# A two-layer MLP with squared ReLU: the first loads and transposes in another order

## The chip, the core and the metric

The kernel runs on one core of a Trainium2 chip. The metric is the device time of one execution in microseconds (us); the figure for a kernel is the median of several runs. The core has five engines that run their own instruction streams side by side: TensorE (PE, matrix products; its weight loads are listed as PEld), VectorE (DVE), ScalarE (ACT), GpSimd (POOL) and SyncE (SP). DMA transfers are issued from the queues of SP, ACT and POOL and are carried by 16 DMA engines. SBUF is the memory on the chip with 128 partitions, PSUM the accumulator memory that PE writes, here eight banks of 512 fp32 columns.

## The reference

```python
B, S, D, F = 1, 2048, 576, 4608      # all inputs bf16
h = jnp.einsum("bsd,df->bsf", x, w1) + b1
r = jnp.where(h > zero, h, zero)
h = r * r
out = jnp.einsum("bsf,fd->bsd", h, w2) + b2
```

x is (1, 2048, 576), w1 is (576, 4608), w2 is (4608, 576).

## The kernel before

**Tiling.** The 2048 rows of x are taken in four blocks of 512 (SB). The hidden dimension F has 36 tiles of 128 (NFT). D = 576 is four full contraction tiles of 128 (NK) and a rest of 64. For the first layer the kernel needs x transposed, so that D lies on the partitions; this is the tile xTw of a block, with nine windows of 64 rows that are held twice, once on each half of the partitions (dup_windows, L117-120, two DVE copies).

**The two ways of the first layer.** Of the 36 hidden tiles, 4 (G) are "full" tiles: a_full computes them with 128-row contractions (w1n, the first 512 columns of w1 in four k tiles of 128 rows) and one step for the last 64 rows of w1 (w1n8), in pairs: the first of a pair on the lower 64 rows of the array, the second on the upper (L202-206). The other 32 are done by a_rows (L179-193) as 16 pairs of 64-row contractions, nine for each, on both halves of the array at once; their weights are w1_h, named w_h in the profile. evac_h (L174-177) finishes a hidden tile: ACT adds b1 and applies ReLU, DVE squares. b1 as a column, b1T, comes from one PE transpose of b1_rows (make_b1T, L164-167).

**The second layer.** phase_t computes the last 128 output columns transposed and turns them by a DMA transpose; phase_b computes the other 448 columns for each 128 rows, adds b2 and stores.

**Order of the work (L309-329).** Block 0: a_full with the order "k_outer", then a_rows. Block 1: a_rows, a_full. Then the second layer of both; then the same for blocks 2 and 3. `keep` holds every instruction to the order of the program on its engine; the order around the start is written out by hand, and each engine takes its instructions strictly in that order.

**The start.** PE runs seven warm-up matmuls on constants (L61-63). Block 0 of x is loaded as four row tiles of 128 x 576 (x_sb, load_x L71-72) and transposed by PE (x_transpose, L145-149), five transposes for each row tile: four of 128 columns, and one of the last 128 columns (E3). PSUM banks hold two halves of 256 rows; x_copies (L151-159) moves them to SBUF on DVE and ACT in turn. SP loads x 0, w1n 0, w1n 1, x 3, w1n 2, w1n 3, then w_h in pieces for the two halves of the partitions (L294-303), with the two w1n8 loads (L77-79) behind the first two pieces. ACT loads x 1 and x 2. POOL makes the identity matrix, zeroes b1_rows and loads b1 and a column of b2 (L94-102).

In a_full's "k_outer" branch (L220-250) matmuls on the halves (`part(h, k)`, L227, four matmuls of 256 columns for the four full tiles) stand between the transposes:

```python
for j in range(2):
    for k in range(NK):
        x_transpose(j, k)
...
x_copies(0)
part(0, 0)
for k in range(NK + 1):
    x_transpose(2, k)
part(0, 1)
part(0, 2)
for k in range(NK + 1):
    x_transpose(3, k)
x_copies(1)
dup_windows(0)
part(0, 3)
part(1, 0)
make_b1T()
```

Then come part(1, 1) to part(1, 3), the two row pairs (L203, L205), and a_rows with L188 and L190.

Of the kernel before, what the change touches and what calls it, by code (L numbers as in the profile page):

```python
# [11 lines left out]
BF16 = mybir.dt.bfloat16  # L12
FP32 = mybir.dt.float32
# [4 lines left out]
def kernel(  # L18
# [9 lines left out]
    nc = tc.nc  # L28
    keep = tc.keep_in_program_order
    P = 128  # L30
    H = 64
    x2 = x.flatten_outer_dims()
    out2 = out.flatten_outer_dims()
    S, D = x2.shape
    F = w1.shape[1]
    NFT = F // P
    NC = D // H
    NK = NC // 2
    G = 4
    GW = G * P  # L40
# [4 lines left out]
    RT = SB // P  # L45
    DT = P
    DM = D - DT

    const = ctx.enter_context(tc.tile_pool(name="const", bufs=1))
    wpool = ctx.enter_context(tc.tile_pool(name="wpool", bufs=1))  # L50
# [5 lines left out]
    ps_h = ctx.enter_context(tc.tile_pool(name="ps_h", bufs=4, space=PSUM))  # L56
    ps_o = ctx.enter_context(tc.tile_pool(name="ps_o", bufs=4, space=PSUM))

    wps = ps_o.tile([P, 512], FP32, name="wps", tag="po")
    ones = nc.const_aps.tensor(1.0, [P, 512], BF16)  # L60
    WARM = [512] * 6 + [128]  # L61
    for i, n in enumerate(WARM):
        keep(nc.tensor.matmul(wps[:, 0:n], lhsT=ones[:, 0:P], rhs=ones[:, 0:n], start=True, stop=True))  # L63

    xs = const.tile([P, RT, D], BF16, name="x_sb")
    w1n = wpool.tile([P, NK, GW], BF16, name="w1n")
    w1n8 = wpool.tile([P, G // 2, P], BF16, name="w1n8")
    w1_h = wpool.tile([P, NC, FH], BF16, name="w1_h")
    w1_v = w1.rearrange("(c p) f -> p c f", p=H)

    def load_x(eng, rt):  # L71
        keep(eng.dma_start(out=xs[:, rt, :], in_=x2[rt * P:(rt + 1) * P, :]))  # L72

    def load_w1n(eng, k):
        keep(eng.dma_start(out=w1n[:, k, :], in_=w1[k * P:(k + 1) * P, 0:GW]))  # L75

    def load_w1n8(eng, h):  # L77
        src = w1[NK * P:D, 0:GW].rearrange("p (i h f) -> p i h f", h=2, f=P)
        keep(eng.dma_start(out=w1n8[h * H:(h + 1) * H, :, :], in_=src[:, :, h, :]))

    def load_w1(eng, h, j0, j1):
        keep(eng.dma_start(out=w1_h[h * H:(h + 1) * H, :, j0 * P:j1 * P],
                      in_=w1_v[:, :, GW + h * FH + j0 * P:GW + h * FH + j1 * P]))

    load_x(nc.sync, 0)
    load_x(nc.scalar, 1)
    load_w1n(nc.sync, 0)
    load_x(nc.scalar, 2)
    load_w1n(nc.sync, 1)
    load_x(nc.sync, 3)  # L90
    for k in range(2, NK):
        load_w1n(nc.sync, k)

    ident = const.tile([P, P], BF16, name="ident")  # L94
    make_identity(nc, ident[:])
    b1_rows = const.tile([P, P], BF16, name="b1_rows")
    nc.gpsimd.memset(b1_rows[:], 0.0)
    nc.gpsimd.dma_start(out=b1_rows[0:NFT, :], in_=b1.rearrange("(ft p) -> ft p", p=P))
    b2_col = const.tile([P, 1], BF16, name="b2_col")
    nc.gpsimd.dma_start(out=b2_col[:], in_=b2[DM:D].rearrange("(d o) -> d o", o=1))  # L100
    b2T = const.tile([P, 1], FP32, name="b2T")
    nc.gpsimd.tensor_copy(out=b2T[:], in_=b2_col[:])
    warm = const.tile([P, 1], FP32, name="warm")
    keep(nc.scalar.activation(out=warm[:], in_=nc.const_aps.tensor(0.0, [P, 1], FP32), func=ACT.Relu))

    E3, O, SPC, E = 0, 1, 5, 6
    LO_W = [O, O + 1, O + 2, O + 3, E, E + 1, E + 2, E3, SPC]
# [20 lines left out]

    w2_sb = wpool.tile([P, NFT, D], BF16, name="w2_sb")
    w2_view = w2.rearrange("(ft p) d -> p ft d", p=P)  # L130
    W2CH = 9

    def load_w2(c):
        keep(nc.sync.dma_start(out=w2_sb[:, c * W2CH:(c + 1) * W2CH, :], in_=w2_view[:, c * W2CH:(c + 1) * W2CH, :]))
# [3 lines left out]
    alloc_xT(0)  # L138
    xT0 = xT_blk[0]
    HS = SB // 2  # L140
    tb_po = [ps_o.tile([P, 2, HS], BF16, name="tb", tag="po") for _ in range(2)]
    tb_ph = [ps_h.tile([P, 2, HS], BF16, name="tb", tag="ph") for _ in range(4)]
    half_banks = [tb_ph, None]

    def x_transpose(j, k):  # L145
        h, q = divmod(j, 2)
        qc = slice(q * P, (q + 1) * P)
        bank, slot, c0 = (half_banks[h][k], 0, k * P) if k < NK else (half_banks[h][2], 1, D - P)
        keep(nc.tensor.transpose(bank[:, slot, qc], xs[:, j, c0:c0 + P], ident[:]))  # L149

    def x_copies(h):  # L151
        hc = slice(h * HS, (h + 1) * HS)
        for k in range(NK):
            src = half_banks[h][k][:, 0, :]
            if k % 2 == 0:
                keep(nc.vector.tensor_copy(out=xT0[:, O + k, hc], in_=src))  # L156
            else:
                keep(nc.scalar.copy(out=xT0[:, O + k, hc], in_=src))  # L158
        keep(nc.vector.tensor_copy(out=xT0[:, E3, hc], in_=half_banks[h][2][:, 1, :]))


    b1T = const.tile([P, NFT], FP32, name="b1T")

    def make_b1T():  # L164
        b1T_ps = ps_o.tile([P, P], BF16, name="b1T_ps", tag="po")
        keep(nc.tensor.transpose(b1T_ps[:], b1_rows[:], ident[:]))  # L166
        keep(nc.vector.tensor_copy(out=b1T[:], in_=b1T_ps[:, 0:NFT]))

# [26 lines left out]
    def a_full(sb, order):  # L195
        xT = xT_blk[sb]
        banks = []
        for g in range(G):
            pool, tag = (ps_o, "po") if g < 2 else (ps_h, "ph")
            banks.append(pool.tile([P, SB], FP32, name="pn", tag=tag))  # L200

        def pair(i, start, stop):  # L202
            keep(nc.tensor.matmul(banks[2 * i][:], lhsT=w1n8[0:H, i, :], rhs=xT[0:H, SPC, :],  # L203
                             start=start, stop=stop, skip_group_check=order == "k_outer"))
            keep(nc.tensor.matmul(banks[2 * i + 1][:], lhsT=w1n8[H:P, i, :], rhs=xT[H:P, E3, :],  # L205
                             start=start, stop=stop, skip_group_check=order == "k_outer"))

        def full(g, k, start, stop):
            keep(nc.tensor.matmul(banks[g][:], lhsT=w1n[:, k, g * P:(g + 1) * P], rhs=xT[:, O + k, :],  # L209
                             start=start, stop=stop))  # L210

        if order == "rows_first":
            for i in (1, 0):
                pair(i, True, False)
            for g in (2, 3, 0, 1):
                for k in range(NK):
                    full(g, k, False, k == NK - 1)
                evac_h(sb, banks[g], g)
        else:
            if order == "k_outer":  # L220
                tb_new = [ps_h.tile([P, 2, HS], BF16, name="tb", tag="ph") for _ in range(2)]
                half_banks[1] = tb_new + tb_po

                def part(h, k):
                    hc = slice(h * HS, (h + 1) * HS)
                    for g in range(G):
                        keep(nc.tensor.matmul(banks[g][:, hc], lhsT=w1n[:, k, g * P:(g + 1) * P],  # L227
                                              rhs=xT[:, O + k, hc], start=(h == 0 and k == 0), stop=False,
                                              skip_group_check=True))

                for j in range(2):
                    for k in range(NK):
                        x_transpose(j, k)
                for j in range(2):
                    x_transpose(j, NK)
                x_copies(0)
                part(0, 0)
                for k in range(NK + 1):
                    x_transpose(2, k)
                part(0, 1)  # L240
                part(0, 2)
                for k in range(NK + 1):
                    x_transpose(3, k)
                x_copies(1)
                dup_windows(0)
                part(0, 3)
                part(1, 0)
                make_b1T()
                for k in range(1, NK):
                    part(1, k)  # L250
            else:
                for g in (2, 3, 0, 1):
                    for k in range(NK):
                        full(g, k, k == 0, False)
            for i in (1, 0):
                pair(i, False, True)
                evac_h(sb, banks[2 * i], 2 * i)
                evac_h(sb, banks[2 * i + 1], 2 * i + 1)
# [35 lines left out]
    for (j0, j1) in [(0, 1), (1, 2), (2, 4), (4, 6), (6, 8), (8, 10), (10, 12)]:  # L294
        load_w1(nc.sync, 0, j0, j1)
        load_w1(nc.sync, 1, j0, j1)
        if j0 == 0:
            load_w1n8(nc.sync, 0)
            load_w1n8(nc.sync, 1)
    load_xT(1)  # L300
    for (j0, j1) in [(12, 14), (14, 16)]:
        load_w1(nc.sync, 0, j0, j1)
        load_w1(nc.sync, 1, j0, j1)
    keep(nc.sync.dma_start(out=b2_bc[:], in_=b2.partition_broadcast(P)))
    for c in (0, 2, 1, 3):
        load_w2(c)
    load_xT(2)

    alloc_hT(0)  # L309
    a_full(0, "k_outer")  # L310
    a_rows(0, 12, 1)
    alloc_hT(1)
# [47 lines left out]
```

## Time and profile before

| | |
|---|---|
| median of 8 runs | 290.93 us (290.62 to 291.45) |
| the profiled execution | 290.9 us, its span 289.1 us |
| PE busy | 285.3 us, 99% of the span |
| DVE, ACT, POOL busy | 78.5, 96.6, 2.2 us |
| first transposes of x (L149) start | 3.73 us |
| first matmul of a_rows (L188) starts | 9.82 us |
| read from HBM, written | 11.36 MB, 2.36 MB |

The landings of the first loads, each from the trace (issue start, us to landing):

| load | queue | issued | to landing |
|---|---|---|---|
| x 0, x 1 | SP, ACT | 0.73, 0.73 | 2.9, 2.8 |
| w1n 0, x 2 | SP, ACT | 1.20, 1.2 | 3.2, 3.0 |
| w1n 1 | SP | 1.69 | 3.9 |
| x 3 | SP | 2.16 | 3.7 |
| w1n 2, w1n 3 | SP | 2.65, 3.12 | 3.6, 3.7 |
| first two w_h pieces | SP | 3.60, 4.3 | 3.5, 3.5 |
| two w1n8 loads | SP | 5.04, 5.7 | 3.0, 2.5 |

How to read the lines: times are microseconds from the start of the span. A line of the timeline gives start, length, engine, line of the kernel, operation, output<-input by the program's names, shape and count. The chain of waits follows the execution back from its last instruction, at each step to what released it; "issue" in it is time in which an engine waited for nothing that the profile shows, and SPq is SP's issuing of a DMA.

### The profile page before, as it was taken

Reading aid. Unit: us, or ns where it says so; the run is one execution under the profiler, and the core shown is the slowest. Engines: PE = TensorE matmul, PEld = TensorE weight load, DVE = VectorE, ACT = ScalarE, POOL = GpSimd, SP = SyncE. Lnnn points to the kernel's source line nnn. Section 1 sums busy time; section 2 is a strip of 40 time slices with the busy share of each in tenths; the row PEclk is TensorE's granted clock in tenths of the full one; section 3 lists DMA queues with packets and bytes.
Section 4 is the critical chain, followed back from the end, with each engine's and each line's share of the span. In section 5 each row is a group of like instructions: output and inputs, shape, how many; then the busy total and the mean of one; then the engine's idle time right before and its main releaser. Section 6 shows DMA issues by size and latency. Waiting matters only on the chain.

```text
span 289.1 us, 4698 instructions
## 1 busy us (share of the span) xinstructions
PE 285.3 (99%) x2032; PEld 139.0 (48%) x2032; DVE 78.5 (27%) x176; ACT 96.6 (33%) x154; POOL 2.2 (1%) x10
## 2 busy tenths in 40 slices
PE   8999999999999999999999999999999999999996
PEld 4544444444444555555544444444444455555555
DVE  1644554444500200000025444444440001100001
ACT  3666666666500000000027666666670000000000
POOL 3000000000000000000000000000000000000000
PEclk9999999999999999999999999999999999999999
DMA  7999999300001100000000000000000110000000
GB/s 198 222 250 195 328 387 207 68 0 2 0 18 30 42 16 18 16 16 18 16 16 2 1 2 0 2 0 2 0 2 0 36 39 16 16 16 20 32 16 18
DMA packets 31605, 16.52 MB, mean 57 GB/s; under 512 B 15700, under 2 KB 31584, under 8 KB 31584
## 3 DMA queue, kind: packets, MB, share of 16 engines
q1 hardware_dynamic: 31232, 15.91, 21.7%
q10 hardware_dynamic: 288, 0.30, 0.4%
q8 instruction: 16, 0.26, 0.4%
q14 instruction: 5, 0.04, 0.0%
q0 software_dynamic: 64, 0.01, 0.0%
HBM read 11.36 MB, written 2.36 MB: 47 GB/s over the span
## 4 chain that ended last, share of the span: by engine, by line
PE 97%; DMA 1%; SPq 1%; issue 0%; DVE 0%
PE ph L188 42%; PE po L289 38%; PE pt L270 11%; PE pn L209 4%; DMA w1n<-in_w_dram 1%; PE pn L227 1%; PE ph L190 1%; PE pn L203 1%; SPq L75 0%; SPq L72 0%; DVE o_sb L291 0%; PE tb L149 0%; PE b1T_ps L166 0%; PE pn L205 0%
## 5 line engine op out<-in xcount | busy, mean ns | idle before, releaser
L188 PE MATMUL ph<-xTw,w_h 64*128 64x512 bf16 x576 | 124.6, 376 | 0.0
L190 PE MATMUL ph<-xTw,w_h 64*128 64x512 bf16 x576 | 124.6, 376 | 0.0
L289 PE MATMUL po<-w_sb,hT 128*128 128x448 bf16 (+2 forms) x612 | 109.4, 341 | 0.0
L176 ACT ACTIVATE r<-ph,b1T 128x512 bf16<-128x512 f32 x128 | 81.0, 684 | 41.7 <-PE ph L190 41.7
L188 PEld LDWEIGHTS <-w_h 64*128 64x128 bf16 x576 | 54.1, 94 | 68.3
L289 PEld LDWEIGHTS <-hT 128*128 128x128 bf16 x612 | 58.5, 98 | 51.0
L177 DVE TENSOR_TENSOR hT<-r 128x512 bf16<-128x512 bf16 x144 | 61.2, 425 | 75.9 <-ACT r L176 75.3
L190 PEld LDWEIGHTS <-w_h 64*128 64x128 bf16 x576 | 54.1, 94 | 0.0
L291 DVE TENSOR_TENSOR o_sb<-po,b_bc 128x448 bf16<-128x448 f32 (+2 forms) x17 | 10.2, 597 | 125.8 <-PE po L289 125.8
L270 PE MATMUL pt<-hT,w_sb 128*128 128x512 bf16 x144 | 31.4, 379 | 0.0
L176 ACT ACTIVATE r<-pn,b1T 128x512 bf16<-128x512 f32 x16 | 10.3, 687 | 61.0 <-PE pn L205 59.6
L270 PEld LDWEIGHTS <-w_sb 128*128 128x128 bf16 x144 | 14.1, 98 | 17.0
L273 ACT ACTIVATE oT<-pt,b2T 128x512 bf16<-128x512 f32 x4 | 2.7, 687 | 28.3 <-PE pt L270 28.3
L209 PE MATMUL pn<-xTw,w1n 128*128 128x512 bf16 x48 | 10.9, 379 | 0.0
L209 PEld LDWEIGHTS <-w1n 128*128 128x128 bf16 x48 | 4.5, 98 | 6.0 <-issue 0.8
L227 PE MATMUL pn<-xTw,w1n 128*128 128x256 bf16 x32 | 4.2, 273 | 0.2
L63 PE MATMUL wps<-const-bfloat16-1.0 128*128 128x512 bf16 (+1 forms) x7 | 2.8, 581 | 0.8 <-PEq L344 0.8
L227 PEld LDWEIGHTS <-w1n 128*128 128x128 bf16 x32 | 2.9, 98 | 1.0 <-DMA w1n<-in_w_dram 0.4
L119 DVE COPY xTw<-xTw 64x2048 bf16<-64x2048 bf16 x4 | 2.8, 690 | 0.2
L156 DVE COPY xTw<-tb 128x256 bf16<-128x256 bf16 x4 | 1.1, 292 | 6.3 <-PE tb L149 6.3
L120 DVE COPY xTw<-xTw 64x2048 bf16<-64x2048 bf16 x4 | 2.8, 688 | 0.1
L158 ACT COPY xTw<-tb 128x256 bf16<-128x256 bf16 x4 | 1.3, 375 | 3.3 <-PE tb L149 3.3
(23 smaller groups left out, 15.2 us busy)
## 6 DMA issues: line engine op xcount, KB each, us to landing
w_sb<-in_w_dram SPq DMA_DIRECT2D x4, 1296.0 KB, 12.0
w_h<-in_w_dram SPq DMA_DIRECT2D x14, 288.0 KB, 6.2
out_dram<-o_sb SPq DMA_DIRECT2D x15, 112.0 KB, 1.7
w_h<-in_w_dram SPq DMA_DIRECT2D x4, 144.0 KB, 3.5
w1n<-in_w_dram SPq DMA_DIRECT2D x4, 128.0 KB, 3.6
out_dram<-ot SPq DMA_DIRECT2D x4, 128.0 KB, 2.0
x_sb<-in_x_dram ACTq DMA_DIRECT2D x2, 144.0 KB, 2.9
x_sb<-in_x_dram SPq DMA_DIRECT2D x2, 144.0 KB, 3.3
```

What stands on the lines that cost most here:

```text
L63: keep(nc.tensor.matmul(wps[:, 0:n], lhsT=ones[:, 0:P], rhs=ones[:, 0:n], start=True, stop=True))
L119: keep(nc.vector.tensor_copy(out=xT[0:H, SPC:SPC + 4, :], in_=xT[H:P, E3:E3 + 4, :]))
L176: keep(nc.scalar.activation(out=r[:], in_=bank[:], func=ACT.Relu, bias=b1T[:, ft:ft + 1], scale=1.0))
L177: keep(nc.vector.tensor_tensor(out=hTs[sb][:, ft, :], in0=r[:], in1=r[:], op=ALU.mult))
L188: keep(nc.tensor.matmul(bx[:], lhsT=w1_h[0:H, LO_C[i], jc], rhs=xT[0:H, LO_W[i], :], start=(i == 0), stop=(i == NC - 1)))
L190: keep(nc.tensor.matmul(by[:], lhsT=w1_h[H:P, UP_C[i], jc], rhs=xT[H:P, UP_W[i], :], start=(i == 0), stop=(i == NC - 1)))
L203: keep(nc.tensor.matmul(banks[2 * i][:], lhsT=w1n8[0:H, i, :], rhs=xT[0:H, SPC, :], start=start, stop=stop, skip_group_check=order == "k_o ...
L209: keep(nc.tensor.matmul(banks[g][:], lhsT=w1n[:, k, g * P:(g + 1) * P], rhs=xT[:, O + k, :], start=start, stop=stop))
L227: keep(nc.tensor.matmul(banks[g][:, hc], lhsT=w1n[:, k, g * P:(g + 1) * P], rhs=xT[:, O + k, hc], start=(h == 0 and k == 0), stop=False, s ...
L270: keep(nc.tensor.matmul(pt[:], lhsT=w2_sb[:, ft, DM:D], rhs=hT[:, ft, :], start=(i == 0), stop=(i == NFT - 1)))
L289: keep(nc.tensor.matmul(po[:, 0:d1 - d0], lhsT=hT[:, ft, jj * P:(jj + 1) * P], rhs=w2_sb[:, ft, d0:d1], start=(i == 0), stop=(i == NFT - 1)))
L291: keep(nc.vector.tensor_tensor(out=o_sb[:, d0:d1], in0=po[:, 0:d1 - d0], in1=b2_bc[:, d0:d1], op=ALU.add))
```

## The change

Loads: x tile 0 comes in two column pieces (columns 0 to 255 on SP, 256 to 575 on ACT), then x 1 and x 3 on SP and x 2 on ACT, then w1n 0 on ACT, w1n 1 on SP, and w1n 2 and 3 in one load on ACT. The 64 rows of w1n8 are loaded once for all 512 columns, by one load on SP whose source repeats the rows for both halves of the partitions. It stands ahead of the w_h pieces; before, two loads stood behind the first two pieces. b1 is loaded on ACT behind the activation that warms up its table, b1_rows is zeroed by DVE, and the column of b2 is loaded on SP, ahead of b2_bc. w2 comes in three pieces of 12 hidden tiles, not four of 9.

PE: one warm-up matmul less; all 20 transposes stand ahead of part(0, 0), with the copies of a bank behind the transposes that fill it. Four transpose banks in ps_h hold several k each; chunk 0's four accumulators are all in ps_o. DVE makes eight of the ten copies, ACT two.

```diff
-    WARM = [512] * 6 + [128]
+    WARM = [512] * 5 + [128]
...
+    def load_w1n8(eng):
+        src = w1[NK * P:D, 0:GW].unsqueeze(0).broadcast_to([2, H, GW])
+        keep(eng.dma_start(out=w1n8[:, :], in_=src))
...
-    load_x(nc.sync, 0)
-    load_x(nc.scalar, 1)
-    load_w1n(nc.sync, 0)
+    b1_rows = const.tile([P, P], BF16, name="b1_rows")
+    nc.vector.memset(b1_rows[:], 0.0)
+    load_x(nc.sync, 0, 0, 2 * P)
+    load_x(nc.scalar, 0, 2 * P, D)
+    load_x(nc.sync, 1)
     load_x(nc.scalar, 2)
-    load_w1n(nc.sync, 1)
     load_x(nc.sync, 3)
-    for k in range(2, NK):
-        load_w1n(nc.sync, k)
+    load_w1n(nc.scalar, 0, 1)
+    load_w1n(nc.sync, 1, 2)
+    load_w1n(nc.scalar, 2, NK)
...
     keep(nc.scalar.activation(out=warm[:], in_=nc.const_aps.tensor(0.0, [P, 1], FP32), func=ACT.Relu))
+    load_w1n8(nc.sync)
+    keep(nc.scalar.dma_start(out=b1_rows[0:NFT, :], in_=b1.rearrange("(ft p) -> ft p", p=P)))
...
-    W2CH = 9
+    W2CH = 12
...
+    tb = [[ps_h.tile([P, 4, HS], BF16, name="tb", tag="ph") for _ in range(2)] for _ in range(2)]
+    PLACE = [(0, 0), (0, 1), (1, 0), (1, 1), (1, 2)]
+    T_ORDER = [0, 1, 2, 3, NK]
+
+    def x_transpose(j):
         h, q = divmod(j, 2)
...
+        for bank, ks in enumerate((T_ORDER[:2], T_ORDER[2:])):
+            for k in ks:
+                slot = PLACE[k][1]
+                c0 = k * P if k < NK else D - P
+                keep(nc.tensor.transpose(tb[h][bank][:, slot, q * P:(q + 1) * P], xs[:, j, c0:c0 + P], ident[:]))
+            for k in ks if q == 1 else ():
+                w = O + k if k < NK else E3
+                copy = nc.scalar.copy if h == 1 and k in (2, 3) else nc.vector.tensor_copy
+                keep(copy(out=xT0[:, w, hc], in_=tb[h][bank][:, PLACE[k][1], :]))
...
+                for j in range(RT):
+                    x_transpose(j)
                 dup_windows(0)
-                part(0, 3)
+                for k in range(NK):
+                    part(0, k)
                 part(1, 0)
                 make_b1T()
...
-        if j0 == 0:
-            load_w1n8(nc.sync, 0)
-            load_w1n8(nc.sync, 1)
     load_xT(1)
...
+    keep(nc.sync.dma_start(out=b2_col[:], in_=b2[DM:D].rearrange("(d o) -> d o", o=1)))
...
-    for c in (0, 2, 1, 3):
+    for c in range(3):
         load_w2(c)
```

## The prediction

> **What bounds the kernel now.** I read the page from its top, then the chain of waits in order of time, then the timeline of the first 12 us, then the DMA landings. The page first:
>
> ```profile
> span 289.1 us, 4698 instructions
> ...
> PE 285.3 (99%) x2032; PEld 139.0 (48%) x2032; DVE 78.5 (27%) x176; ACT 96.6 (33%) x154; POOL 2.2 (1%) x10
> ...
> PE 97%; DMA 1%; SPq 1%; issue 0%; DVE 0%
> ```
>
> The chain that ended last is 97% TensorE. From the first matmul of a_rows (L188) to the end the tensor engine doesn't wait, and the change leaves that work as it is. So the change is worth what it does to one instant: when L188 starts. The chain of waits up to there (start, length, what):
>
> ```profile
> 2.65 3.62 DMA w1n<-in_w_dram
> 6.27 0.05 issue
> 6.32 0.61 PE pn L227 x4
> 6.92 0.28 PE tb L149 x5
> 7.20 0.87 PE pn L227 x8
> 8.08 0.06 PE b1T_ps L166
> 8.13 1.31 PE pn L227 x12
> 9.44 0.32 PE pn L203
> ```
>
> The last wait ends at 6.27, when the third tile of w1n lands (issued fifth on SP, at 2.65). After it PE runs through without a pause, and the timeline gives the instant itself:
>
> ```profile
> 9.38 0.39 PE L203 MATMUL pn<-xTw,w1n 64*128 64x512 bf16 x1
> 9.82 0.38 PE L188 MATMUL ph<-xTw,w_h 64*128 64x512 bf16 x1
> ```
>
> L188 starts at 9.82. Its first two weights, both 147 KB pieces of w_h, were issued at 3.60 and 4.3 and took 3.5 us each to land: 7.1 and 7.8. They have 2 us to spare. Last, the same stretch by quarter microseconds (the last two numbers are the busy share of the 16 DMA engines and GB/s):
>
> ```profile
> 5.00:5.25 0.25, 0.25 (x5) 0.19 (x2) 0.21 (x2) 0.15 (x1) 0.00 (x0) 1.00 1.02 340
> 5.25:5.50 0.25, 0.25 (x7) 0.23 (x4) 0.00 (x0) 0.00 (x0) 0.00 (x0) 1.00 0.99 329
> ```
>
> The engines are full here with w1n rows of 1024 bytes. In the packet records of the trace the middle packet of an engine lasts 51 ns for 1152 bytes, 46 ns for 1024, 18 ns for 256; for 512 bytes the mean is 34 ns. I use these below as the price of one packet on one engine. Summing the quarters, x and the four w1n tiles (590 + 524 = 1114 KB) had moved by 5.75; the last w1n tile is known as landed at 3.12 + 3.7 = 6.8. The same sum for the first two w_h pieces gives 6.33 and 7.1 against 7.1 and 7.8. So landing follows the last byte by 0.7 to 1.05 us. I take 0.7, that of w_h.
>
> **What the Trainium skill says.**
> 1. "DMA: Bandwidth & Descriptors", section "Why a DMA increments its semaphore by 16 and not by 1": a transfer is spread over the largest number of engines, at most 16, that divides the slowest dimension of both sides. Its section "Rules for kernel authors" names this case: a leading zero-stride broadcast of c copies "confines the whole DMA to at most c engines". All loads of this trace have 64 or more rows outermost (b1 has 36), so it neither supports nor contradicts this.
> 2. The same page, "Queues, rings and completion order": each engine takes turns between the queues it has work for, packet by packet, and in order within one. The trace fits: packets of SP's and ACT's queues interleave between 2.5 and 3.75.
> 3. The same page, "Issuing engines are not separate DMA queues": a second issuing engine saves issue time alone. The trace agrees on the issue time, 0.39 to 0.46 us for an x tile on either.
> 4. "TensorE: Matmul & The Clock Gate", Part 1: the array starts at half clock and is released after some 3.4 us of activity. The trace agrees: warm-up matmuls of 512 columns start 0.43 us apart, later ones 0.21.
>
> **The change, part by part.**
>
> *Order of loads.* Before, SP issues seven loads (x, w1n) up to 3.55, ACT two. After, each issues four: x in full by 2.0, w1n by about 2.5. The stream has the same 1114 KB. By 2.5 the engines have moved 129 KB (sum of the quarters); at the 360 GB/s that they hold from 2.5 to 3.5, the rest takes 985/360 = 2.74 us: 5.25 instead of 5.75, if nothing else is in the way.
>
> *Warm-up.* One matmul of 0.43 us less: it ends near 3.2, about when the pieces of x tile 0 land (0.73 + 2.4, an estimate from 147 KB at 2.56 plus 0.55). Nothing on the path.
>
> *Transposes and copies.* The same 20 transposes (0.28 us per five in the chain) stand ahead of chunk 0; the last x tile moves at about 4.1 and lands at 4.8, against 5.9 before, so they end at 5.1. Eight copies on DVE at 0.285 us, two on ACT at 0.33, then two duplications at 0.69: DVE is done at 4.0 + 8 x 0.285 + 1.4 = 7.7, before 9.25. Off the path.
>
> *w1n8 in one broadcast load.* The source is now 2 x 64 rows with a zero stride outermost, the destination 128 rows. By point 1 it runs on two engines: 64 rows of 1024 bytes each, 64 x 46 ns = 2.94 us of work on these two, where the old pair of loads put 4 KB on each engine. It is fifth on SP, and the w_h pieces queue behind it on those same two engines. This is the disputed cost. From below: the skill's rate for an engine (Specifications, 27 GiB/s) gives 65.5 KB / 29 = 2.3 us. From above: the rate of 256-byte packets, 14.2 GB/s, gives 4.6 us. Not below zero in this case, as the bytes on those engines grow. I take 2.94.
>
> Now the two engines. From 2.5 they still have x (32 packets x 51 ns = 1.63, less 0.36 moved, plus 0.05 for the split tile), w1n 32 x 46 = 1.47, w1n8 2.94: done at 2.5 + 1.32 + 1.47 + 2.94 = 8.23. Then the first two w_h pieces, 36 packets of 256 bytes each: 72 x 18 = 1.30, at 9.53; landed at 10.23.
>
> And PE. While w1n8 (SP's queue) and the last w1n load (ACT's, 16 KB an engine) take turns there, this load ends at about 6.1 instead of 5.25 on the two engines, and lands at 6.8 to 7.0. Behind it are 24 matmuls at 0.109 (12 took 1.31) and the b1 transpose: 2.7 us, so L203 at about 9.6; w1n8 itself has landed at 8.9. The four row matmuls take 0.44: PE would start L188 at 10.0. The weights come at 10.23. With 0.05 for the semaphore L188 starts at 10.3: **0.46 later than 9.82**.
>
> *Later weights.* The next pair is done at 9.53 + 1.30 = 10.83 and landed at 11.5, wanted at 10.3 + 1.94 = 12.2. The (2,4) pair: 72 x 34 ns = 2.4, landed at 14.0, wanted at 14.2. Just in time (before: 13.4 against 13.7); no stall counted, up to 0.4 in the range.
>
> *b1 and b2.* b1 moves from POOL to ACT behind four issues (to 2.5), the table load (1.28) and the warm activation (0.20): issued at 4.2, landed at 7.0 to 7.6 (2.8 to 3.4 us as other small loads). PE wants it after 20 of 32 matmuls, at 8.2. Covered by 0.6; without that it would stall PE by what is missing. The memset goes to an idle DVE, b2's column to SP ahead of w2, used at 76 us: zero. w2 in three pieces: 324 x 4 KB as before, wanted at 76 us, landed by 47: zero.
>
> *Banks.* Four ps_o banks for chunk 0 and four ps_h for transposes: a_rows finds ps_h free as the copies are done at 6.3; its third pair waits for ACT's evictions as before.
>
> **Sum.** 290.9 (the profiled execution's own time, span 289.1) + 0.46 = **291.4**; the median 290.93 is the same number. That is within 0.2% (0.58 us), about what a measurement of this kernel can tell from no change, leaning to slower.
>
> **The rivals.**
> - *The load is spread over all 16 engines after all* (a builder that reshapes the source, or the rule not binding here). Then w1n lands at 5.25 + 0.7 = 5.95, the chain of 2.7 puts L203 at 8.65 and L188 at 9.1, w_h has landed at 7.6: -0.7, **290.2**. For it: nothing in the trace shows a load on fewer engines. Against: the skill names just this form. Chance 22%.
> - *The two engines are slower still*: w1n8 halfway to its upper price, 3.8 us instead of 2.94. Everything behind it on these engines comes 0.86 later, L188 starts at 11.15: +1.33, **292.2** (293.1 at the full 4.6). It ends as slower as soon as a packet lasts over 48 ns (64 x 2 ns is what is left to 0.58). For it: some packets between 3.75 and 4.75 last 330 ns. Against: the middle one keeps to 46. Chance 20%.
> - *The clock*: PE has idle stretches from 3.2 to 5, with one warm-up matmul less; if the array is released a window later, some 3 us run at half speed: 24 matmuls cost up to 1.3 more, partly in the shadow of the w_h wait. L188 at 10.9: **291.9**. Against: 2.4 us of solid warm-up. Chance 10%.
>
> **How the numbers follow.** The forecast has 48%, its own range 291.0 to 292.0 (w1n8 from 2.6 to 3.2 us, lag 0.7 to 1.05). Half of the first rival lies below 290.2, some 40% of the second above 292.5: the range is 290.2 to 292.5. Faster: 2% of the forecast and 65% of the first rival, 0.15. Slower: 45% of the forecast, the second rival, 90% of the third, 0.50. Same: the rest, 0.35.
>
> **What would show it.** Right: w1n8's landing over 5 us after its issue; L188 starting near 10.3 behind a wait on w_h; x tile 3 landed before 5. Wrong: w1n8 landing within 3.5 us (first rival); a wait on w_h again at the third pair, or past 11 (second); matmuls of L227 over 0.2 us apart (third); a wait of PE on b1_rows, which I count at nothing.

## The result and the profile after

The changed kernel takes 292.15 us (median of 11 runs, 291.75 to 292.97), the kernel before 290.88 in the same comparison (30 runs). The ratio is 1.0044, with a 95% interval of 1.0035 to 1.0053: slower by 1.0 to 1.5 us. That lies in the stated range (290.2 to 292.5), but above the forecast of 291.4 and above its own range (291.0 to 292.0).

The page of the changed kernel (the profiled execution took 291.87 us):

```profile
span 290.1 us, 4695 instructions
...
PE 284.8 (98%) x2031; PEld 138.9 (48%) x2031; DVE 79.0 (27%) x179; ACT 95.9 (33%) x152; POOL 1.0 (0%) x7
...
PE 96%; DMA 3%; SPq 0%; DVE 0%; issue 0%
```

PE is busy for half a microsecond less (one warm-up matmul), and the span is 1.0 us longer: waiting was added. The chain of waits up to a_rows (start, length, what) says where:

```profile
4.17 4.72 DMA b_rows<-in_b_dram
8.88 0.05 issue
8.93 0.23 PE b1T_ps L160
9.16 1.31 PE pn L218 x12
10.47 0.32 PE pn L197
```

Before, the last wait of this chain was w1n 2, ended at 6.27. Now it is b1: 9 KB, issued at 4.17 and landed at 8.88. The timeline has the wait in square brackets, and the first matmul of a_rows (now L182):

```profile
8.93 0.23 PE L160 MATMUL b1T_ps<-ident,b_rows 128*128 128x128 bf16 x1 [1.01 <-DMA b_rows<-in_b_dram]
10.85 0.38 PE L182 MATMUL ph<-xTw,w_h 64*128 64x512 bf16 x1
```

L182 starts at 10.85, 1.03 later than L188 before. From there to the end the two spans agree within 0.03 us (290.1 - 10.85 = 279.25; 289.1 - 9.82 = 279.28). So all of the profiled loss lies ahead of a_rows, and the wait for b1 is as long as this loss, 1.01 us: without it L182 would start at 9.84 (an estimate, 10.85 - 1.01, if nothing else were late).

Why does so small a load take 4.7 us? The DMA view of the changed kernel, cut to two stretches. First 6.5 to 8.1 (q1 is SP's queue, q10 ACT's; packets, MB, share of the 16 engines):

```profile
DMA packets 1103, 0.33 MB, mean 208 GB/s; under 512 B 1027, under 2 KB 1103, under 8 KB 1103
...
q1 hardware_dynamic: 1103, 0.33, 84.3%
```

Then 8.1 to 8.4:

```profile
q1 hardware_dynamic: 61, 0.02, 23.5%
q10 hardware_dynamic: 8, 0.00, 2.6%
```

In the first stretch nearly all packets are rows of w_h, of 256 bytes; ACT's queue, which has nothing left but the rest of b1, moves nothing for these 1.6 us. Then it moves eight packets, six of b1 and two of 4 bytes. In the packet records 30 of b1's 36 packets of 256 bytes moved from 5.62 to 6.45, and the last six from 8.12 to 8.27. b1 has 36 rows, so by the Trainium skill's rule ("DMA: Bandwidth & Descriptors", section "Why a DMA increments its semaphore by 16 and not by 1") it goes over 12 engines, three rows each: six packets are the share of two engines. The trace's landing records agree. A load of x there has 16 entries, which I read as one for each engine that carried a share of it. b1 has twelve (after an early one at 5.06), ten of them by 6.92 and the last two at 8.81 and 8.88. w1n8 has two (after an early one at 4.11), at 8.63 and 8.70. The first w_h piece, behind it on SP, has 14 by 7.45, and its last two only at 9.25 and 9.30. So w1n8 ran on two engines, and what had rows on them came late.

The 1024-byte packets of SP's queue, which after 5.5 are w1n8's, come in this time at 47 in a microsecond: two every 42 ns. As each lasts 46 ns, their times overlap and add up to 2.2 engines. The last three move between 8.13 and 8.21, among b1's six.

### The profile page after: what moved, and what is told of

Same layout as the page of the kernel before. It is cut to its first block, busy times and chain, and to the rows that moved or that the text cites. A ratio compares the mean times of both kernels' runs of the same rounds, so it can differ in the third digit from the quotient of the medians.

```text
span 290.1 us, 4695 instructions
## 1 busy us (share of the span) xinstructions
PE 284.8 (98%) x2031; PEld 138.9 (48%) x2031; DVE 79.0 (27%) x179; ACT 95.9 (33%) x152; POOL 1.0 (0%) x7
## 4 chain that ended last, share of the span: by engine, by line
PE 96%; DMA 3%; SPq 0%; DVE 0%; issue 0%
PE ph L182 42%; PE po L269 38%; PE pt L250 11%; PE pn L203 4%; DMA b_rows<-in_b_dram 2%; DMA x_sb<-in_x_dram 1%; PE ph L184 1%; PE pn L197 1%; PE pn L218 0%; SPq L72 0%; DVE o_sb L271 0%; PE tb L150 0%; PE b1T_ps L160 0%; PE pn L199 0%
## 5 line engine op out<-in xcount | busy, mean ns | idle before, releaser
L182 PE MATMUL ph<-xTw,w_h 64*128 64x512 bf16 x576 | 124.6, 376 | 0.0
L182 PEld LDWEIGHTS <-w_h 64*128 64x128 bf16 x576 | 54.1, 94 | 68.3
L170 ACT ACTIVATE r<-pn,b1T 128x512 bf16<-128x512 f32 x16 | 10.3, 687 | 63.3 <-PE pn L199 62.0
L154 DVE COPY xTw<-tb 128x256 bf16<-128x256 bf16 x8 | 1.9, 285 | 4.0 <-PE tb L150 3.6
L150 PE MATMUL tb<-ident,x_sb 128*128 128x128 bf16 x20 | 1.9, 244 | 0.9 <-DMA x_sb<-in_x_dram 0.9
```

Of the source, the lines that this page charges most:

```text
L170: keep(nc.scalar.activation(out=r[:], in_=bank[:], func=ACT.Relu, bias=b1T[:, ft:ft + 1], scale=1.0))
L182: keep(nc.tensor.matmul(bx[:], lhsT=w1_h[0:H, LO_C[i], jc], rhs=xT[0:H, LO_W[i], :], start=(i == 0), stop=(i == NC - 1)))
```

## The experiments

**b1 held behind the w1n8 load, or something else?** Four runs, each against the kernel before. First, b1 issued from POOL as before the change:

```diff
-    keep(nc.scalar.dma_start(out=b1_rows[0:NFT, :], in_=...))
+    nc.gpsimd.dma_start(out=b1_rows[0:NFT, :], in_=...)
```

> The kernel after, with the load of b1 issued from POOL again, as before the change. Theory A (b1's packets are held on the two engines that carry the w1n8 load, and PE waits for b1): the wait of 1.0 us at the b1 transpose goes, the first a_rows matmul starts at 9.8 to 9.9 in place of 10.85, and the time falls by 0.9 to 1.0 us, to a ratio of 1.000 to 1.001 against the kernel before. Theory B (the forecast's own: the w_h pieces queued behind w1n8 set the start): the start stays within 0.3 us of 10.85. Theory C (moving all transposes ahead is what costs): no change, ratio 1.004.

Measured: the wait for b1 is gone, but the time isn't: 292.67 us (8 runs, 291.41 to 295.57), ratio 1.0066 (1.0037 to 1.0095). The single executions spread over 4 us; the best is 0.3 below the changed kernel's best. By the median the expectation is missed. The profiled execution is the slowest, where PE comes to b1 only at 11.86, so it says little of that wait; the spread is taken up below.

Second, two plain loads for w1n8:

```diff
-        src = w1[NK * P:D, 0:GW].unsqueeze(0).broadcast_to([2, H, GW])
-        keep(eng.dma_start(out=w1n8[:, :], in_=src))
+        for h in range(2):
+            keep(eng.dma_start(out=w1n8[h * H:(h + 1) * H, :], in_=w1[NK * P:D, 0:GW]))
```

> The kernel after, with the one w1n8 load replaced by two plain loads of 64 rows, one for each half of the partitions; b1 stays on ACT. Theory A (two engines hold b1 back): w1n8 lands within 3.5 us of its issue, b1 within 3.4 us (by 7.6), no wait at the b1 transpose, first a_rows matmul at 9.8, time down by 1.0 us, ratio 1.000 to 1.001. Rival D (b1 is late because ACT issues it late, behind four loads and the table load): b1 still lands at 8.5 or later, start at 10.5 or later, ratio 1.003 or more.

Measured: b1, still on ACT, is no longer waited for, and its 36 packets move from 5.46 to 6.55 with no long gap. It lands at 7.72, 3.8 us after its issue; the two loads, each with 16 entries in the landing records, land 4.5 and 4.2 us after theirs, all somewhat later than expected. So ACT's late issue isn't the cause (rival D, b1 at 8.5 or later, falls). But the time is 293.04 (8 runs, 291.01 to 295.08), ratio 1.0069 (1.0036 to 1.0102): again a spread, from 0.7 below the changed kernel's best to 2 us above its worst.

Third, b1 issued on ACT ahead of the table's warm-up:

```diff
+    keep(nc.scalar.dma_start(out=b1_rows[0:NFT, :], in_=...))
     keep(nc.scalar.activation(out=warm[:], ...))
     load_w1n8(nc.sync)
-    keep(nc.scalar.dma_start(out=b1_rows[0:NFT, :], in_=...))
```

> The kernel after, with b1 issued on ACT ahead of the table's warm-up, so at 2.6 and ahead of the w1n8 load (3.03), in place of 4.17. Theory A: b1's packets enter the two engines ahead of w1n8's, it lands by 6.0, and the gain is the same 0.9 to 1.0 us as with b1 on POOL. If the packets of the two queues really took turns one by one, b1 would not have been held in the first place, and this edit would bring at most the 1.57 us of its earlier issue, which also ends the wait of 1.0: so only the landing tells (before 6.0 in A, 7.3 where the same 4.7 us pass).

Measured: PE no longer waits for b1, and yet 291.86 us (5 runs, 291.72 to 291.98), ratio 1.0039 (1.0027 to 1.0051): not the gain of 0.9 expected, and the intervals overlap with the changed kernel's. The timeline of its weight loads shows what came in place of that wait:

```profile
9.36 0.09 PEld L197 LDWEIGHTS <-w1n 64*128 64x128 bf16 x1 [0.53 <-DMA w1n<-in_w_dram]
9.95 0.09 PEld L182 LDWEIGHTS <-w_h 64*128 64x128 bf16 x1 [0.47 <-DMA w_h<-in_w_dram]
10.44 0.09 PEld L184 LDWEIGHTS <-w_h 64*128 64x128 bf16 x1 [0.40 <-DMA w_h<-in_w_dram]
14.60 0.09 PEld L184 LDWEIGHTS <-w_h 64*128 64x128 bf16 x1 [0.59 <-DMA w_h<-in_w_dram]
```

b1 is issued at 2.89, just ahead of w1n8, its packets move from 5.24 to 5.81 with no long gap, and it lands at 6.4: between the 6.0 of theory A and the 7.3 of a landing that still takes 4.7 us. But now PE waits for w1n8 itself, for both first w_h pieces, and at the third pair once more. The forecast had the second w_h piece at 10.23 and L188 at 10.3, and this run has that wait, up to 10.44. It doesn't show that the wait for b1 hid it in the changed kernel: there w1n8 and the two pieces landed earlier (8.70, 9.30 and 9.74, against 9.32, 9.91 and 10.40 here, where SP also issued the first piece 0.43 later). So the early b1 took one wait away and brought others.

Fourth, the broadcast load alone, put into the kernel before in place of its two loads:

```diff
         if j0 == 0:
-            load_w1n8(nc.sync, 0)
-            load_w1n8(nc.sync, 1)
+            load_w1n8(nc.sync)      # one load, source repeated for both halves
```

> The kernel before with one edit of the change alone: the w1n8 rows in one load with a repeated source, at the place of the two old loads (SP, issue at 5.0, behind the first w_h pieces). Two engines: it lands at about 10.7 (7.1 when the engines reach it, 64 x 46 ns, 0.7 to land), the row pair waits for it, the first a_rows matmul starts near 11.1 in place of 9.82, ratio 1.004 to 1.005. Sixteen engines: it lands by 8.2, nothing waits, ratio 1.000.

Measured: 293.17 us (6 runs, 292.55 to 295.67), ratio 1.0102 (1.0072 to 1.0132): the sign and the place are those of two engines, the size at the median is more than twice. The timeline of the slowest execution:

```profile
12.27 0.41 PE L203 MATMUL pn<-xTw,w1n 64*128 64x512 bf16 x1 [2.85 <-DMA w1n<-in_w_dram]
12.90 0.63 PE L188 MATMUL ph<-xTw,w_h 64*128 64x512 bf16 x1
```

The row pair waits 2.85 us for a load of 131 KB. Its first packets move at 6.9, but only from 8.5 do two come every 42 ns; the last ends at 11.25, and the load has landed at 12.22, not at 10.7 as worked out. And there is a cost that was not expected: matmuls of 512 columns that last 0.38 us elsewhere last 0.63 here. The stretch from 12 to 14 in that kernel (the third number from the end is the granted clock):

```profile
12.00:14.00 2.00, 1.73 (x10) 0.70 (x12) 0.43 (x1) 1.29 (x3) 0.00 (x0) 0.63 0.79 210
```

The trace's records of the granted clock have it at half from 12.51 to 15.92. The Trainium skill ("TensorE: Matmul & The Clock Gate", Part 1) says that an idle window of about 3.4 us does this; here a wait of 2.85 us was enough. Two of the six executions, this one among them, have a mean granted clock of 0.993 or 0.994 in place of 1.0; the other four (292.55 to 293.44) took their loss without such a cut.

**The same load twice.** If w1n8 on its two engines is what holds b1 and w_h, more of it must hold them longer. The w1n8 load made twice, the second into a tile that nothing reads:

```diff
     load_w1n8(nc.sync)
+    w1n8x = wpool.tile([P, GW], BF16, name="w1n8x")
+    keep(nc.sync.dma_start(out=w1n8x[:, :], in_=w1[NK * P:D, 0:GW].unsqueeze(0).broadcast_to([2, H, GW])))
```

> The kernel after with the w1n8 load made twice, the second time into a tile that nothing reads, directly behind the first. Theory A: the two engines have 2.94 us more to do ahead of b1 and w_h, b1 lands at 11.8 in place of 8.9, L182 starts at 13.7 to 13.8: 295.0 us, ratio 1.014; PE then stands for 3.9 us, so that a stretch at half clock may come on top, up to 1.7 us more. If the load ran on all 16 engines, 131 KB more would take 0.4 us: ratio 1.004 to 1.006.

Measured: 294.54 us (5 runs), ratio 1.0136 (1.0112 to 1.0160), as two engines give it and far from the 1.004 to 1.006 of sixteen. From 8.0 to 8.5 this kernel moves w1n8 rows and nothing else, which is the cleanest view of the load:

```profile
DMA packets 24, 0.02 MB, mean 49 GB/s; under 512 B 0, under 2 KB 24, under 8 KB 24
...
q1 hardware_dynamic: 24, 0.02, 13.8%
```

13.8% of 16 engines is 2.2 engines: again two packets of 46 ns every 42 ns, 49 GB/s in all. The way there was another than expected, though: b1 lands at 9.6 and not at 11.8 (its last six packets move from 8.57 to 9.15, with 110 of the two loads' 256 rows still to go), and the larger part of the added delay is then w_h, which PE waits for until 12.76 and 13.16.

**The spread.** Why do the kernels with b1 on POOL and with two plain loads vary by 4 us? In the profiled executions PE's speed differs: these are 20 matmuls of 256 columns, in the run with two plain loads (292.74 us), then 16 of them in the run of the next paragraph (290.99 us).

```profile
5.97 3.91 PE L218 MATMUL pn<-xTw,w1n 128*128 128x256 bf16 x20
```

```profile
6.15 1.97 PE L218 MATMUL pn<-xTw,w1n 128*128 128x256 bf16 x16 [0.21 <-DVE xTw L154]
9.86 0.38 PE L182 MATMUL ph<-xTw,w_h 64*128 64x512 bf16 x1
```

That is 0.20 us for each against 0.12; the changed kernel's profiled execution has 2.35 us for 20. The records of the granted clock say why: full clock from 9.17 us on in the first of these runs, but from 4.25 in the second, 3.56 in the changed kernel and 4.24 in the kernel before. L182 starts at 11.62 and at 9.86, 1.76 apart; the times of the two executions are 1.75 apart. In the slowest execution with b1 on POOL (295.57 us) the full clock comes at 13.03 and the 20 take 4.47 us; but there x tile 3 is late as well, 7.04 where the changed kernel has 5.23, because of two of its 16 engines (the other 14 entries are in by 5.26; one packet of x took 1.67 us, where the middle one takes 51 ns). So a transfer has its part in that one. The test: two plain loads, and two warm-up matmuls more than the changed kernel, so that PE has no pause ahead of its transposes.

```diff
-    WARM = [512] * 5 + [128]
+    WARM = [512] * 7 + [128]
```

> The kernel after with the two plain w1n8 loads and seven warm-up matmuls of 512 columns in place of five, so that PE has work without a pause from 0.8 until the third x tile is transposed. Theory E (with the w1n8 load mended, what makes single executions up to 4 us longer is the tensor clock, released a window of 3.4 us or two later when PE pauses early): the spread of 291.0 to 295.1 shrinks to under 1 us, with the median at 290.8 to 291.3. Rival (the spread is the transfers', x tile 3 landing late): the spread stays over 2 us.

Measured: 291.18 us (13 runs, 290.77 to 292.79), ratio 1.0016 (1.0003 to 1.0029). Eleven of the 13 lie at 291.76 or below, where five of eight were above 292.7. But two are at 292.57 and 292.79, so the spread is 2.0 us, not under 1 as theory E had it: the longer warm-up takes most of the spread away, and what makes the rest isn't shown. L182 starts at 9.86, without a wait for b1 or w_h. And the same warm-up in the changed kernel, its one w1n8 load kept:

> The kernel after with seven warm-up matmuls of 512 columns in place of five, the one w1n8 load kept. It differs from the run with two plain w1n8 loads and seven warm-ups (291.18 us) in that load alone. Theory A (b1 is held behind w1n8 on its two engines): the wait at the b1 transpose stays, L182 starts near 10.85, 291.9 to 292.2 us, ratio 1.0035 to 1.0045, so 0.8 to 1.0 us above that run. If the clock was what made the kernel after slow: 291.2, ratio 1.001.

Measured: 292.25 us (5 runs, 291.89 to 292.51), ratio 1.0044 (1.0030 to 1.0058). The wait for b1 stays, and L182 starts at 10.89:

```profile
8.98 0.23 PE L160 MATMUL b1T_ps<-ident,b_rows 128*128 128x128 bf16 x1 [1.05 <-DMA b_rows<-in_b_dram]
10.89 0.38 PE L182 MATMUL ph<-xTw,w_h 64*128 64x512 bf16 x1
```

Both profiled executions have the full clock early (from 4.25 and 3.92), and the two kernels differ in the w1n8 load alone. So its one-load form costs 292.25 - 291.18 = 1.07 us, or 1.00 if each is taken against the kernel before of its own comparison. That is most of the loss of the change, and the clock isn't its cause. With five warm-up matmuls the medians don't show it: where the profile shows a late clock in the kernel with two plain loads, it costs 1.76, more than the wait. Why the changed kernel, with the same five, varies by 1.2 us only is open. In part the wait may hide a late clock: with the clock of the 292.74 us execution PE would come to b1 at 9.71 in place of 8.93, which is 0.8 us later and not 1.8 (an estimate). The reverse test, the kernel before with one warm-up matmul less:

> The kernel before with five warm-up matmuls of 512 columns in place of six. Theory E: the pause ahead of the first x tile grows from 0.1 to 0.5 us, and a part of the executions gets the full clock a window later: most at 290.8, some at 292 to 293. If one warm-up matmul is nothing by itself, as the forecast had it: ratio 1.000 and no wider than before (290.4 to 291.4).

Measured: 291.22 us (13 runs, 290.69 to 291.78), ratio 1.0011 (1.0003 to 1.0020): some 0.3 us, but no execution at 292, where theory E had expected some. The missing warm-up matmul alone doesn't make the spread. The next two runs have a pause of PE later on.

**The other parts alone.** The kernel before with the change's loads of x and w1n:

```diff
-    load_x(nc.sync, 0)
-    load_x(nc.scalar, 1)
-    load_w1n(nc.sync, 0)
...
+    load_x(nc.sync, 0, 0, 2 * P)
+    load_x(nc.scalar, 0, 2 * P, D)
+    load_x(nc.sync, 1)
...
+    load_w1n(nc.scalar, 0, 1)
+    load_w1n(nc.sync, 1, 2)
+    load_w1n(nc.scalar, 2, NK)
```

> The kernel before with the change's order of the loads of x and w1n alone (x tile 0 in two pieces, x first, w1n over both queues in three loads); the w1n8 loads, b1, the warm-up and PE's order stay. As forecast for the loads: the last w1n tiles land at 6.0 to 6.3 and both at once, PE starts its last run of matmuls up to 0.3 us earlier, L188 at 9.5 to 9.8, ratio 0.999 to 1.000. If x tile 3 or w1n 0 comes later than before: 1.001 to 1.002.

Measured: 293.25 us (10 runs, 291.50 to 294.56), ratio 1.0069 (1.0044 to 1.0094). With PE's old order the first part needs w1n 0 right behind two x tiles, and it now lands behind all of x:

```profile
5.66 0.61 PE L228 MATMUL pn<-xTw,w1n 128*128 128x256 bf16 x4 [1.35 <-DMA w1n<-in_w_dram]
```

A pause of 1.35 us in the first 6 us, and the spread is back, 3.1 us. Three of the ten executions have a mean granted clock of 0.994, which none of the kernel before has. The profiled one (291.63) is one of the fast, so what the slow ones did is not shown. Then the change's order on PE alone:

```diff
-                for j in range(2):
-                    for k in range(NK):
-                        x_transpose(j, k)
...
+                for j in range(RT):
+                    x_transpose(j)
                 dup_windows(0)
-                part(0, 3)
+                for k in range(NK):
+                    part(0, k)
```

> The kernel before with the change's order on PE alone: all transposes ahead of chunk 0, with its banks and copies; loads, warm-up, b1 and w1n8 stay. PE stands from 4.9 until x tile 3 lands at 5.9, then does 5 transposes and 32 matmuls (0.28 + 3.5 us) and the b1 transpose: L188 at 10.2 in place of 9.82, ratio 1.001 to 1.002; with theory E the pause of 1 us adds executions of 292 and more, where the window falls badly.

Measured: 291.20 us (21 runs, 290.80 to 293.58), ratio 1.0014 (1.0005 to 1.0024), a ratio as expected: PE stands 0.99 us for x tile 3, until 6.25. Of the executions of 292 and more that theory E added, there is one in 21. So a pause by itself does not bring the spread.

**A version that beats both?** The kernel before with its own loads spread over both queues:

```diff
     load_x(nc.sync, 0)
     load_x(nc.scalar, 1)
     load_w1n(nc.sync, 0)
     load_x(nc.scalar, 2)
     load_w1n(nc.sync, 1)
+    load_w1n(nc.scalar, 2)
     load_x(nc.sync, 3)
-    for k in range(2, NK):
-        load_w1n(nc.sync, k)
+    load_w1n(nc.scalar, 3)
```

> The kernel before with its loads of x and w1n spread over both queues in the order of use: SP x 0, w1n 0, w1n 1, x 3; ACT x 1, x 2, w1n 2, w1n 3. All else stays. The third w1n tile, whose landing at 6.27 ends the last wait of the kernel before, is issued at 1.7 in place of 2.65. If it then lands 0.3 to 0.5 us earlier, L188 starts at 9.4 to 9.6 and the time is 290.5, ratio 0.9985 to 0.9995. If the 16 engines, not SP's issuing, set that landing, nothing changes: 1.000. If w1n 1 comes later for sharing the engines: 1.001.

Measured: 290.96 us (13 runs, 290.54 to 291.77), ratio 1.0000 (0.9991 to 1.0009). The start did come as hoped, and was given back at the third pair:

```profile
9.34 0.38 PE L188 MATMUL ph<-xTw,w_h 64*128 64x512 bf16 x1
13.55 0.09 PEld L190 LDWEIGHTS <-w_h 64*128 64x128 bf16 x1 [0.44 <-DMA w_h<-in_w_dram]
```

0.48 us were won and 0.44 lost. Last, the two w1n8 issues taken off SP, so that w_h follows sooner:

```diff
-        if j0 == 0:
-            load_w1n8(nc.sync, 0)
-            load_w1n8(nc.sync, 1)
...
                 x_copies(0)
+                load_w1n8(nc.scalar, 0)
+                load_w1n8(nc.scalar, 1)
```

> The kernel before with its x and w1n loads spread over both queues, as in the run before this, and the two w1n8 loads issued from ACT behind its first copies, not from SP. In that run L188 started at 9.34 (0.48 earlier than in the kernel before), and PE lost 0.44 of it again at the third pair, waiting for w_h, while the 16 engines were half idle from 6 to 10 for want of issued loads. Theory F (SP's issuing of w_h is the next bound): without the two w1n8 issues (1.29 us) on SP all later w_h pieces are issued 1.3 us earlier, the wait at the third pair goes, 290.5 us, ratio 0.998 to 0.999. Rival: the engines, not SP, set the landing of w_h: the wait stays, ratio 1.000.

Measured: 319.6 us (6 runs), ratio 1.0990 (1.0950 to 1.1030), for a reason that has nothing to do with either theory. From the list of waits of this kernel (in total, times, longest):

```profile
ACT xTw L158 <- DMA w_h<-in_w_dram: 26.3, 1, 26.3
```

The two issues on ACT stand behind the w_h loads in the program. ACT's next copies come 26.3 us late, put down to the landing of one of these loads, and PE stands 24.1 us behind them. Why ACT waits for that load isn't shown. Whether SP's issuing is the next bound stays open.

## Why the prediction was right and where it failed

The measured 292.15 lies inside the stated range, but by luck. That end of the range came from the second rival (slower engines, 292.2), and its slower engines did not come: w1n8's rows ended at 8.21, where the forecast had 8.23. The wait that put the time there is the wait for b1, which the forecast counted at nothing and listed as a sign of being wrong.

- **The instant that matters**: right. The loss of the profiled execution is L182's 1.03 us and nothing behind it.
- **w1n8 on two engines**: right, and the core of the loss: its landing has two entries, and it landed 5.7 us after its issue, over the 5 of the forecast's sign. Its rows began 0.2 us later than worked out (5.45, not 5.29) and passed faster, one every 42 ns on an engine and not 46, which cancels. The first rival (all 16 engines, chance 22%) falls. Its time of 290.2 was too low besides: with two plain loads and the full clock early L182 starts at 9.86, not 9.1, as w1n 1 holds PE until 6.15 with 28 matmuls still to go, where the rival let it wait for w1n 2 and 3 alone with 24.
- **w_h behind it on the same engines**: the mechanism is right (the last two shares of the first piece landed 1.8 us after the others, and the run with b1 early waits up to 10.44), but it isn't what ends last in the changed kernel: there the two pieces land at 9.3 and 9.7, forecast 10.23.
- **b1**: this is the step that failed. It was put at "landed at 7.0 to 7.6", "Covered by 0.6". It landed at 8.88, PE wanted it at 7.92, and the wait was 1.01. The issue time (4.17, forecast 4.2) was right; the error was to price b1 as a small load by itself, when a sixth of its rows travel on the two engines that w1n8 fills. The forecast reasoned so for w_h and for w1n, and not for b1.
- **Taking turns**: the second point from the Trainium skill ("DMA: Bandwidth & Descriptors", "Queues, rings and completion order") was used as if each packet of ACT's queue had to wait for one of SP's. Where packets of both queues meet the trace agrees: with the load made twice b1's start at 8.57, 8.63 and 8.68, and rows of w1n8 at 8.59, 8.64 and 8.70. But b1's last six packets met them late: they stood for 1.7 us while SP's went, and moved when w1n8 was all but done, or in the run with the load made twice with 110 rows still to go. And ACT's large w1n load wasn't slowed (landed at 6.3, forecast 6.8 to 7.0). What lets a queue's packets in is open.
- **x tile 3** landed at 5.23, forecast 4.8; PE had nothing to do for 0.66 us ahead of it.
- **The warm-up** was put at nothing; alone, in the kernel before, it is 0.3 us (0.1 to 0.6). The third rival, the clock, is real in other versions (1.76 us between the two executions above), but not what made this kernel slow: seven warm-ups left it at 292.25.
- A slip on which nothing rests: before, SP issues six loads of x and w1n, not seven.

Sum: 0.46 us were forecast, 1.03 measured in the profiled execution, 1.27 between the medians. The first two differ by 0.57: the start of a_rows was to be set by w_h, at 10.3, and b1's late landing set it at 10.85. The last 0.24 is the spread of executions, whose cause in this kernel no profile here shows.

## What to carry to other kernels

Look at the outermost dimension of both sides of every load: a repeat of two in front put the whole load on two engines here. Then price everything that has rows on those engines, from any queue, the smallest load included. When several loads are late for one cause, moving one of them can bring the next wait and little gain, as with b1 issued early: undo the common cause. At the start of a kernel look at when the full clock comes: it came at 3.6 us in one execution here and at 9.2 in another, and that cost more than the wait that had been removed.

## What the runs showed of the hardware

- A load whose source repeats 64 rows twice ran on two engines, at 49 GB/s, with two entries in the landing records. Two loads of the same rows, one for each half, had 16 each.
- Six packets of another queue stood for 1.7 us on these two engines; the 30 others of the same load moved between 5.62 and 6.45.
- After a wait of 2.85 us the tensor clock was at half for 3.4 us (from 12.51 to 15.92).
- The full clock came at 3.56 to 4.25 us in the profiled executions of the two kernels compared and of the one with two plain loads and seven warm-ups; at 9.17 with two plain loads and five, where 20 matmuls took 3.91 us and not 2.35.
- With two plain loads single executions spread over 4.1 us with five warm-up matmuls, over 2.0 with seven.
